# Splitting fp32 PE transposes into two 64-partition row tiles in a fused RG-LRU and soft-MoE kernel

## The chip, the cores and the metric

The kernel runs on one core of a Trainium2 chip (trn2). The metric is the device time of one execution in microseconds (us), on that core. A run gives one time; the median of several runs stands for a kernel. A profiled execution gives a trace beside it, whose span (first to last instruction) is a little shorter than the time.

## The reference

Everything is fp32. B, S, D = 4, 5056, 256, so there are 20224 tokens of 256 features; E = 8 experts with 4 slots each (32 slots) and a hidden width of 1024.

```
sig_r = sigmoid(r_gate);  sig_i = sigmoid(i_gate)
a_t   = exp(8 * sig_r * log(clip(sigmoid(a_param))))        # per token and feature
xg    = sqrt(max(1 - a_t*a_t, 1e-6)) * sig_i * x
h[t]  = a_t[t] * h[t-1] + xg[t];  y = h                     # scan over S, per batch row
logits = y @ phi                                            # 20224 x 32
slot_in = softmax(logits over tokens).T @ y                 # 32 x 256
slot_out[e] = relu(slot_in[e] @ w1[e]) @ w2[e]              # 4 slots of each expert
out = softmax(logits over slots) @ slot_out                 # 20224 x 256
```

## The kernel before

Tokens are taken in quads of 512 (40 of them, the last is half) and units of two quads (21 units, the first and the last of one quad). Loads bring a quad with tokens on partitions: partition p holds 4 consecutive tokens, 4 KB. The scan needs features on partitions and time along the free axis, so three kinds of PE transposes through an identity stand between the layouts:

- **TR** (`mk_sr`, line 857): the gate r of a quad, 8 transposes of 128x128 into a two-bank PSUM tile `pair`; ACT then computes tanh from it into the SBUF tile `A` (**SR**, line 868).
- **TU** (`mk_scan`, line 1013): u, the gated x of a unit, one feature half h at a time, 8 transposes (16 in the units marked E, where i and x are added up in PSUM) into a `pair`; DVE multiplies it by the norm in place (**ST**, line 1030) and scans (**SC**, line 1047), which writes y over `A`.
- **TY** (`mk_y`, line 1073): y back to tokens on partitions, 8 transposes a quad into a `pair`, copied by ACT (line 1087) or DVE (line 1089) to the SBUF tile `yn` (**YC**). The quads 37 to 39 go through `mk_yh` (line 1103) and quad 29 through one bank at a time.

Each transpose is one weight load (the data are the stationary operand) and one matmul (the identity streams): 128 columns in both. In the trace `pair<-ident,st` and `pair<-ident,b` at these three lines are the transposes; a `pair` is one of three, `one` is a single bank.

Other work on PE: **LG** (logits, line 1153), **TE/TF** (transposed logits, line 1197 and 1223), **AC** (slot sums, line 1251), **CT** (line 1627), **SP** and **DN** (slot inputs and denominators, lines 1474 and 1488), **L1/L2** (experts, lines 1529 and 1577), **HP/OT** (output, lines 1693 and 1721), and **WU**, fillers of two transposes of the identity (line 1402) which the planner puts where its plan has PE idle. ACT also does the gates' tanh or sigmoid **SI** (lines 907 and 909), **EX** (exp, line 975), **RT** (square root, line 994) and the exponentials of the softmax. POOL multiplies (lines 937 and 957). SP queues every load and store.

The order of tasks on each engine is a table of names, `ORDER`, walked by `run_fixed`, which keeps a clock with modelled durations only to give out buffers, to interleave the emission and to place fillers. So a task waits for the one before it on its engine, for its inputs, and for its buffer.

Of the kernel before, what the change touches and what calls it, by code (L numbers as in the profile page):

```python
# [16 lines left out]
P = 128  # L17
J = 4
# [138 lines left out]
COLD = 5.5  # L157
PEL = 0.21
# [424 lines left out]
def kernel(  # L583
# [188 lines left out]
    def load(nm, q):  # L772
# [5 lines left out]
        def emit():  # L778
            rows = src[nm][q * QT : q * QT + n * P, :].rearrange("(p n) d -> p (n d)", n=n)
# [63 lines left out]

    def mk_sr(q):
# [18 lines left out]
        tr = add("PE", f"TR{q}", 0.05 + 0.2182 * n, deps=[ld[("r", q)], t_const], prio=q - TRP, emit=e_tr,  # L863
                 alloc=[rp], uses=[st[("r", q)]], shape="T")
# [135 lines left out]
    def mk_scan(p):  # L1000
        c = plen(p)
        tok0 = quads(p)[0] * QT
        for h in range(H):
            up = Buf("pair", f"up{p}.{h}")

            def e_tu(h=h, up=up):
                for i, q in enumerate(quads(p)):
                    n = qlen(q) // P
                    o = inv(t(up)[:, i, : n * P], n)
                    nms = ("i", "x") if gate_of(q) == "E" else ("x",)  # L1010
                    for nm in nms:
                        for m in range(n):
                            nc.tensor.matmul(  # L1013
                                o[:, m, :],
                                raw(nm, q)[:, m * D + h * P : m * D + (h + 1) * P],
                                ident, is_transpose=True, start=(nm == nms[0] and m == 0), stop=(nm == nms[-1]),
                                skip_group_check=True,
                            )

            nt = 2 if gate_of(quads(p)[0]) == "E" else 1  # L1020
            tu = add("PE", f"TU{p}.{h}", 0.04 + 0.1091 * c / P * nt, deps=[U[q] for q in quads(p)], prio=pos_u(p) - TUP + h * 0.1,
                     emit=e_tu, alloc=[up], uses=[st[(nm, q)] for q in quads(p) for nm in (("x", "i") if nt == 2 else ("x",))],
                     shape="T")

            def flat(up=up):
                return t(up).rearrange("p a b -> p (a b)")
# [29 lines left out]
    def mk_y(q):  # L1056
# [6 lines left out]
        for b0 in range(0, qlen(q) // P, step):  # L1063
            yp = Buf("pair" if q in YP4 else ONE, f"yp{q}.{b0}")
# [726 lines left out]
```

## Time and profile before

| what | value |
|---|---|
| time, median of 3 runs | 288.57 us (287.92 to 288.71) |
| profiled execution, span | 286.4 us |
| busy PE / DVE / ACT / POOL | 257.5 / 229.0 / 238.8 / 192.7 us |
| DMA moved | 100.05 MB, mean 349 GB/s |
| mean granted PE clock | 0.988 |

The profiled execution was not timed apart from its span, so the median is the time that it is set beside: 2.2 us lie outside the span (288.57 - 286.4). The run has four stretches: gates, scan and everything behind them until about 207 us, the close of the softmax over tokens until 214, the experts (L1, L2) until 232, and the output until 286. Busy time on PE is the time covered by its matmuls, whose ends are modelled; spacing from one start to the next tells more. An engine's idle time is put down to what released it last.

### The profile page before, as it was taken

Reading aid. Unit: us, or ns where it says so; the run is one execution under the profiler, and the core shown is the slowest. Engines: PE = TensorE matmul, PEld = TensorE weight load, DVE = VectorE, ACT = ScalarE, POOL = GpSimd, SP = SyncE. Lnnn points to the kernel's source line nnn. Section 1 sums busy time; section 2 is a strip of 40 time slices with the busy share of each in tenths; the row PEclk is TensorE's granted clock in tenths of the full one; section 3 lists DMA queues with packets and bytes.
Section 4 is the critical chain, followed back from the end, with each engine's and each line's share of the span. In section 5 each row is a group of like instructions: output and inputs, shape, how many; then the busy total and the mean of one; then the engine's idle time right before and its main releaser. Section 6 shows DMA issues by size and latency. Waiting matters only on the chain.

```text
span 286.4 us, 6221 instructions
## 1 busy us (share of the span) xinstructions
PE 257.5 (90%) x2455; PEld 196.3 (69%) x2455; DVE 229.0 (80%) x269; ACT 238.8 (83%) x253; POOL 192.7 (67%) x148
## 2 busy tenths in 40 slices
PE   8889899989999879869998999999999999999850
PEld 7888767877767657556977766676765578777640
DVE  0148749999999899999999999999965558886730
ACT  7799999999999999999999999999542069955440
POOL 5198997999999999989999999993010511310100
PEclk9999999999999999999999999999999999999995
DMA  6999999999999929976999998799996039999996
GB/s 227 387 412 404 402 410 366 403 414 408 407 406 410 403 96 378 412 272 241 338 410 355 380 323 332 252 364 392 399 408 256 3 128 414 420 412 418 414 406 289
DMA packets 27409, 100.05 MB, mean 349 GB/s; under 512 B 3058, under 2 KB 3060, under 8 KB 24948
## 3 DMA queue, kind: packets, MB, share of 16 engines
q1 hardware_dynamic: 27376, 99.66, 89.0%
q8 instruction: 19, 0.31, 0.4%
q14 instruction: 10, 0.08, 0.1%
q10 hardware_dynamic: 4, 0.00, 0.0%
HBM read 78.94 MB, written 20.71 MB: 348 GB/s over the span
## 4 chain that ended last, share of the span: by engine, by line
PE 38%; ACT 19%; DMA 14%; DVE 13%; issue 9%; POOL 3%; SPq 2%; ACTq 0%; POOLq 0%; DVEq 0%
DMA st<-in_r_gate_dram 10%; PE bank L1721 6%; PE pair L1013 5%; ACT b L868 5%; ACT b L994 5%; PE pair L1073 4%; DVE b L1047 4%; DVE pair L1030 4%; ACT b L909 4%; DMA b<-in_x_dram 4%; PE one L1251 3%; PE bank L1529 3%; PE one L1577 2%; PE one L1153 2%; PE pair L857 2%
## 5 line engine op out<-in xcount | busy, mean ns | idle before, releaser
L1047 DVE TENSOR_TENSOR_SCAN b<-b,pair 128x1024 f32<-128x1024 f32 (+8 forms) x48 | 93.1, 1951 | 0.7
L937 POOL TENSOR_TENSOR b<-b 128x1024 f32<-128x1024 f32 x38 | 89.8, 2398 | 3.9 <-ACT b L909 2.8
L957 POOL TENSOR_TENSOR b<-b 128x1024 f32<-128x1024 f32 (+2 forms) x39 | 71.2, 1864 | 10.6 <-ACT b L975 10.6
L1013 PE MATMUL pair<-ident,b 128*128 128x128 f32 x412 | 52.5, 275 | 5.7 <-DVE b L1047 2.8
L1030 DVE SCALAR_TENSOR_TENSOR pair<-b,pair 128x1024 f32<-128x1024 f32 (+2 forms) x42 | 48.1, 1154 | 6.9 <-issue 2.9
L1013 PEld LDWEIGHTS pair<-ident,b 128*128 128x128 f32 x412 | 45.1, 140 | 11.8 <-DVE yn L1089 3.3
L857 PE MATMUL pair<-ident,st 128*128 128x128 f32 x308 | 40.7, 277 | 4.8 <-DMA st<-in_r_gate_dram 2.4
L975 ACT ACTIVATE b<-b,ca 128x2048 f32<-128x2048 f32 (+3 forms) x24 | 42.8, 1803 | 0.0
L1655 POOL TENSOR_TENSOR b<-b,rs_all 128x512 f32<-128x512 f32 (+3 forms) x12 | 10.6, 895 | 47.5 <-DVE rs_all L1650 17.7
L1073 PE MATMUL pair<-ident,b 128*128 128x128 f32 x288 | 38.8, 278 | 4.1 <-ACT b L868 1.9
L857 PEld LDWEIGHTS pair<-ident,st 128*128 128x128 f32 x308 | 33.7, 141 | 11.4 <-ACT b L868 5.1
L1073 PEld LDWEIGHTS pair<-ident,b 128*128 128x128 f32 x288 | 31.3, 140 | 13.3 <-DVE b L1047 3.2
L868 ACT ACTIVATE b<-pair 128x1024 f32<-128x1024 f32 (+1 forms) x39 | 38.3, 1010 | 1.7 <-PE pair L857 1.5
L1089 DVE COPY yn<-pair 128x1024 f32<-128x1024 f32 x23 | 27.7, 1206 | 3.0 <-PE pair L1073 3.0
L1735 ACT COPY b<-bank 128x512 f32<-128x512 f32 x35 | 19.5, 611 | 12.7 <-PE bank L1721 9.3
L1721 PE MATMUL bank<-eS,yn 32*128 32x256 f32 x238 | 27.2, 406 | 2.0 <-ACT b L1735 0.9
L994 ACT ACTIVATE b<-b 128x2048 f32<-128x2048 f32 (+1 forms) x14 | 25.2, 1820 | 0.0
L1721 PEld LDWEIGHTS bank<-eS,yn 32*128 32x128 f32 x238 | 19.3, 197 | 5.6 <-ACT b L1735 1.6
L909 ACT ACTIVATE b<-b 128x2048 f32<-128x2048 f32 x12 | 22.9, 1917 | 0.0
L1251 PE MATMUL one<-yn,eS 128*32 128x257 f32 x296 | 22.3, 385 | 0.0
L1153 PE MATMUL one<-b,phi_sb 128*32 128x512 f32 (+1 forms) x164 | 20.9, 579 | 0.0
L1737 DVE COPY b<-bank 128x512 f32<-128x512 f32 x22 | 14.4, 679 | 8.1 <-PE bank L1721 4.5
(152 smaller groups left out, 375.0 us busy)
## 6 DMA issues: line engine op xcount, KB each, us to landing
b<-in_x_dram SPq DMA_DIRECT2D x39, 512.0 KB, 9.1
st<-in_r_gate_dram SPq DMA_DIRECT2D x38, 512.0 KB, 8.1
b<-in_i_gate_dram SPq DMA_DIRECT2D x38, 512.0 KB, 7.7
out_dram<-b SPq DMA_DIRECT2D x19, 1024.0 KB, 6.9
b<-in_moe_w_dram SPq DMA_DIRECT2D x28, 512.0 KB, 7.5
st<-in_moe_w_dram SPq DMA_DIRECT2D x4, 512.0 KB, 6.0
st<-in_r_gate_dram SPq DMA_DIRECT2D x3, 256.0 KB, 2.8
st<-in_i_gate_dram SPq DMA_DIRECT2D x1, 512.0 KB, 6.3
```

The costliest lines, as they stand in the source:

```text
L857: nc.tensor.transpose(out=o[:, m, :], in_=raw("r", q)[:, m * D + h * P : m * D + (h + 1) * P], identity=ident,)
L868: nc.scalar.activation(dst, t(rp)[:, :, :c], AF.Sigmoid if SIGR else AF.Tanh, scale=1.0 if SIGR else 0.5)
L909: nc.scalar.activation(v, v, AF.Tanh, scale=0.5)
L937: eng.tensor_tensor(out=o, in0=a, in1=b, op=ALU.mult)
L957: eng.tensor_tensor(out=o, in0=v, in1=v, op=ALU.mult)
L975: nc.scalar.activation(v, v, AF.Exp, scale=ca[:, h : h + 1], bias=ca[:, h : h + 1])
L994: nc.scalar.activation(v, v, AF.Sqrt, bias=quarter if f != 1.0 else f, scale=-f)
L1013: nc.tensor.matmul(o[:, m, :], raw(nm, q)[:, m * D + h * P : m * D + (h + 1) * P], ident, is_transpose=True, start=(nm == nms[0] and m == ...
L1030: nc.vector.scalar_tensor_tensor(v, t(Nb[p])[:, h, :c], 0.5e-3 if gate_of(quads(p)[0]) == "E" else 1e-3, v, op0=ALU.max, op1=ALU.mult)
L1047: nc.vector.tensor_tensor_scan(dst, dst, flat()[:, s0:s1], init, op0=ALU.mult, op1=ALU.add)
L1073: nc.tensor.transpose(out=flat()[:, b * D + h * P : b * D + (h + 1) * P], in_=tokens(q, b0 + b, 1)(h), identity=ident,)
L1721: nc.tensor.matmul(t(ops[x])[:, c * D : (c + 1) * D], t(hT)[r, off : off + (P - 1) * ns + 1 : ns], t(soRb)[r, :D], start=True, stop=True,)
```

## The change

Each transpose of TR (but quad 0), TU and TY (but the quads in single banks) becomes two: the upper 64 partitions of the data against a 64x64 identity, and the lower 64, one after the other, each writing 64 columns. The two halves go to different banks of the `pair`. To make that possible, layouts move: in a unit of two quads, x and i are loaded with 8 tokens to a partition (a quad's load takes 4 of them, so 4 KB out of every 8 KB); ACT's SR and the copies YC read and write with one more dimension; and `yn` holds the features in the order (f, h, k) in place of (h, f, k), so SP is split into matmuls that write 64 partitions each and waits for both halves of the last update of `accS` (AE11a and AE11b) in place of the first alone. Engine orders in `ORDER` are the same; the planner's modelled durations differ, so fillers and buffers move.

```
+TT = 0.0655
+HP = 64
...
-            rows = src[nm][q * QT : q * QT + n * P, :].rearrange("(p n) d -> p (n d)", n=n)
+            if nm != "r" and len(quads(p)) == 2:
+                u0 = quads(p)[0] * QT
+                rows = src[nm][u0 : u0 + plen(p), :].rearrange("(p n) d -> p (n d)", n=2 * J)[:, i * J * D : (i + 1) * J * D]
+            else:
+                rows = src[nm][q * QT : q * QT + n * P, :].rearrange("(p n) d -> p (n d)", n=n)
...
+    def rowtiles(in_):
+        for f in range(2):
+            k = slice(f * HP, (f + 1) * HP)
+            yield f, in_[k], ident[k, k]
...
             for h in range(H):
-                o = inv(t(rp)[:, h, :c], n)
+                o = [inv(t(rp)[:, f, h * c // 2 : (h + 1) * c // 2], n) for f in range(2)]
                 for m in range(n):
-                    nc.tensor.transpose(
-                        out=o[:, m, :],
-                        in_=raw("r", q)[:, m * D + h * P : m * D + (h + 1) * P],
-                        identity=ident,
-                    )
+                    for f, v, idn in rowtiles(raw("r", q)[:, m * D + h * P : m * D + (h + 1) * P]):
+                        nc.tensor.transpose(out=o[f][:, m, :], in_=v, identity=idn)
...
         def e_sr():
-            dst = t(A[p])[:, :, i * QT : i * QT + c]
-            nc.scalar.activation(dst, t(rp)[:, :, :c], AF.Sigmoid if SIGR else AF.Tanh, scale=1.0 if SIGR else 0.5)
+            dst = t(A[p])[:, :, i * QT : i * QT + c].rearrange("q h (f x) -> q h f x", f=2)
+            v = t(rp)[:, :, :c].rearrange("q f (h x) -> q h f x", h=H)
+            nc.scalar.activation(dst, v, AF.Sigmoid if SIGR else AF.Tanh, scale=1.0 if SIGR else 0.5)
...
+                n = c // P
+                o = [inv(t(up)[:, 0, QT - c // 2 :], n), inv(t(up)[:, 1, : c // 2], n)]
...
+                            for f, v, idn in rowtiles(raw(nm, q)[:, m * D + h * P : m * D + (h + 1) * P]):
+                                nc.tensor.matmul(
+                                    o[f][:, i * J + m, :], v, idn, is_transpose=True,
...
+                        for f, v, idn in rowtiles(tokens(q, b0 + b, 1)(h)):
+                            nc.tensor.transpose(out=t(yp)[:, f, (b * H + h) * HP : (b * H + h + 1) * HP], in_=v, identity=idn)
...
+                if wide:
+                    dst = dst.rearrange("p j (f d) -> p f j d", f=2)
+                    v = t(yp)[:, :, : nb * P].rearrange("p f (j d) -> p f j d", d=P)
...
         def e_sp(h):
-            nc.tensor.matmul(
-                t(sp)[:, h * NS : (h + 1) * NS], accS[:, h * P : (h + 1) * P], small["W"][:, 0, :],
-                start=True, stop=True,
-            )
-
-        a = add("PE", "SP0", 0.26, deps=[w, AE["a"]], prio=-60, alloc=[sp], emit=lambda: e_sp(0), shape="M")
+            for f in range(2):
+                nc.tensor.matmul(
+                    t(sp)[f * HP : (f + 1) * HP, h * NS : (h + 1) * NS],
+                    accS[:, f * P + h * HP : f * P + (h + 1) * HP], small["W"][:, 0, :], start=True, stop=True,
+                )
+
+        a = add("PE", "SP0", 0.26, deps=[w, AE["a"], AE["b"]], prio=-60, alloc=[sp], emit=lambda: e_sp(0), shape="M")
```

PE near the start, from TR0 (`one<-ident,st`, two halves) over TR1 to TR2; `pair<-ident` and `one<-ident` without a second name are fillers. Before:

```order
L882 MATMUL one_78<-ident,st_61 128x128 x4
L1402 MATMUL pair_83<-ident 128x128 x2
L1402 MATMUL pair_84<-ident 128x128 x2
L857 MATMUL pair_82<-ident,st_62 128x128 x8
L1402 MATMUL one_77<-ident 128x128 x2
L1402 MATMUL pair_83<-ident 128x128 x2
L1402 MATMUL one_78<-ident 128x128 x2
L857 MATMUL pair_84<-ident,st_63 128x128 x8
```

and with the change:

```order
L892 MATMUL one_78<-ident,st_61 128x128 x4
L1418 MATMUL pair_83<-ident 128x128 x2
L1418 MATMUL pair_84<-ident 128x128 x2
L870 MATMUL pair_82<-ident,st_62 128x64 x16
L1418 MATMUL one_77<-ident 128x128 x2
L1418 MATMUL pair_83<-ident 128x128 x2
L1418 MATMUL one_78<-ident 128x128 x2
L1418 MATMUL pair_84<-ident 128x128 x2
L870 MATMUL pair_83<-ident,st_63 128x64 x16
```

Eight transposes have become sixteen of half the height, and one more filler stands ahead of TR2.

PE at the close of the softmax over tokens, from the last AC over CT3, SP0, DN, SP1 and CT4 to L1 (`yn,eS` is AC, `ident,b` CT, `W,accS` SP, `accS,W` DN, `b,yn` L1). Before:

```order
L1251 MATMUL bank_2142<-yn_70,eS_76 32x257 x2
L1627 MATMUL bank_2146<-ident,b 128x4x32 x4
L1474 MATMUL one_77<-W,accS 128x32
L1488 MATMUL one_77<-accS,W 128x1
L1474 MATMUL one_77<-W,accS 128x32
L1627 MATMUL bank_2141<-ident,b 128x4x32 x4
L1529 MATMUL bank_2145<-b,yn_71 32x256 x32
```

and with the change:

```order
L1267 MATMUL bank_3184<-yn_70,eS_76 32x257 x2
L1644 MATMUL bank_3188<-ident,b 128x4x32 x4
L1491 MATMUL one_78<-W,accS 64x32 x2
L1505 MATMUL one_78<-accS,W 128x1
L1491 MATMUL one_78<-W,accS 64x32 x2
L1644 MATMUL bank_3183<-ident,b 128x4x32 x4
L1546 MATMUL bank_3187<-b,yn_71 32x256 x32
```

SP0 and SP1 have become two matmuls of 64 output partitions each, on either side of DN, which keeps 128. Up to there the whole list of PE changes its tile shape 120 times in place of 58 and holds 67 fillers in place of 54.

## Rows read from the trace of the kernel before

**Rows 1.** Busy us of PE, PEld, DVE, ACT, POOL by stretch; clock, DMA share, GB/s

```profile
10.00:201.00 191.00, 176.80 (x1572) 136.83 (x1572) 172.85 (x142) 190.25 (x154) 175.50 (x97) 1.00 0.94 362
201.00:214.40 13.40, 13.38 (x148) 9.43 (x140) 10.48 (x26) 7.27 (x13) 1.69 (x3) 1.00 1.03 404
...
232.00:286.40 54.40, 41.77 (x423) 32.68 (x419) 35.51 (x74) 31.41 (x67) 6.11 (x7) 0.94 0.93 382
```

**Rows 2.** What ACT waited for, 9 to 206 us: total us, times, longest

```profile
ACT yn L1087 <- PE pair L1073: 1.5, 1, 1.5
ACT b L868 <- PE pair L857: 1.5, 1, 1.5
```

**Rows 3.** What DVE waited for, 43 to 208 us

```profile
DVE pair L1030 <- ACT b L994: 1.3, 3, 0.8
DVE pair L1030 <- PE pair L1013: 1.1, 4, 0.4
```

**Rows 4.** Groups of PE transposes: shapes, count, busy us, mean ns, idle before

```profile
L1013 PE MATMUL pair<-ident,b 128*128 128x128 f32 x412 | 52.5, 275 | 5.7 <-DVE b L1047 2.8 <-DVE yn L1089 1.7 <-ACT b L868 0.9
L857 PE MATMUL pair<-ident,st 128*128 128x128 f32 x308 | 40.7, 277 | 4.8 <-DMA st<-in_r_gate_dram 2.4 <-ACT b L868 1.5 <-DVE b L1047 0.4
L1073 PE MATMUL pair<-ident,b 128*128 128x128 f32 x288 | 38.8, 278 | 4.1 <-ACT b L868 1.9 <-DVE b L1047 1.7 <-ACT yn L1087 0.3
```

**Rows 5.** One TY within the chain that ended last: start, us on the chain

```profile
182.42 0.87 PE pair L1073 x8
```

**Rows 6.** Timeline of PE: four transposes of 32 partitions, and what follows

```profile
39.20 0.43 PE L1197 MATMUL one<-ident,b 32*128 32x32 f32 x4
39.56 1.42 PE L1013 MATMUL pair<-ident,b 128*128 128x128 f32 x11
```

**Rows 7.** The same transposes on line 1197: ns min/median/max, and their loads' timeline

```profile
L1197 PE MATMUL one<-ident,b x32: 221/273/330, 39.2 to 175.0; 128*128 128x128 f32 x28, 32*128 32x32 f32 x4
39.20 0.32 PEld L1197 LDWEIGHTS one<-ident,b 32*128 32x128 f32 x4 [0.17 <-issue]
```

**Rows 8.** Weight loads of OT: four loads into four row tiles; their group

```profile
243.09 0.21 PEld L1721 LDWEIGHTS bank<-eS,yn 32*128 32x128 f32 x4 [0.27 <-DVE b L1737]
L1721 PEld LDWEIGHTS bank<-eS,yn 32*128 32x128 f32 x238 | 19.3, 197 | 5.6 <-ACT b L1735 1.6 <-DVE b L1641 1.1 <-ACT yn L1704 1.0
```

**Rows 9.** Timeline near the start: PE's TR2 and ACT's SR2

```profile
8.88 1.09 PE L857 MATMUL pair<-ident,st 128*128 128x128 f32 x8 [0.91 <-DMA st<-in_r_gate_dram]
10.01 1.03 ACT L868 ACTIVATE b<-pair 128x1024 f32<-128x1024 f32 x1 [1.46 <-PE pair L857]
```

**Rows 10.** Timeline at the end of the scans: DVE's ST19, SC20; PE's LG11

```profile
196.96 2.36 DVE L1030 SCALAR_TENSOR_TENSOR pair<-b,pair 128x1024 f32<-128x1024 f32 x2 [0.34 <-PE pair L1013]
206.34 0.75 DVE L1047 TENSOR_TENSOR_SCAN b<-b,pair 128x256 f32<-128x256 f32 x1
207.19 0.52 PE L1153 MATMUL bank<-b,phi_sb 128*32 128x128 f32 x6
```

**Rows 11.** Timeline of the close: DVE's AE11, PE's SP0, DN, SP1, CT4, L1

```profile
212.68 0.61 DVE L1285 SCALAR_TENSOR_TENSOR accS<-accS,dm,bank 128x128 f32<-128x128 f32 x2 [0.50 <-PE bank L1251]
213.15 0.34 PE L1474 MATMUL one<-W,accS 128*128 128x32 f32 x2
213.35 0.38 PE L1488 MATMUL one<-accS,W 128*128 128x1 f32 x2
213.59 0.39 PE L1474 MATMUL one<-W,accS 128*128 128x32 f32 x2
213.81 0.70 PE L1627 MATMUL bank<-ident,b 128*128 128x128 f32 x4
214.45 0.42 PE L1529 MATMUL bank<-b,yn 128*32 128x256 f32 x4
```

**Rows 12.** ACT reading PSUM: SR from 9 us on, and SR0 in pieces of two

```profile
L868 ACT ACTIVATE b<-pair x38: 602/1021/1062, 10.0 to 175.1; 128x1024 f32<-128x1024 f32 x37, 128x512 f32<-128x512 f32 x1
L892 ACT ACTIVATE b<-one 128x512 f32<-128x512 f32 x2 | 1.3, 634 | 0.1
```

More of the change, by code (lines that the diff above doesn't have):

```diff
@@ L1006, in e_tu @@
             def e_tu(h=h, up=up):
+                n = c // P
+                o = [inv(t(up)[:, 0, QT - c // 2 :], n), inv(t(up)[:, 1, : c // 2], n)]
                 for i, q in enumerate(quads(p)):
[L1008 to L1009 removed]
                     nms = ("i", "x") if gate_of(q) == "E" else ("x",)
                     for nm in nms:
[L1012 to L1018 removed]
+                        for m in range(qlen(q) // P):
+                            for f, v, idn in rowtiles(raw(nm, q)[:, m * D + h * P : m * D + (h + 1) * P]):
+                                nc.tensor.matmul(
+                                    o[f][:, i * J + m, :], v, idn, is_transpose=True,
+                                    start=(nm == nms[0] and m == 0 and i == 0), stop=(nm == nms[-1]),
+                                    skip_group_check=True,
+                                )
             nt = 2 if gate_of(quads(p)[0]) == "E" else 1
[L1021 removed]
+            tu = add("PE", f"TU{p}.{h}", 0.04 + TT * c / P * nt, deps=[U[q] for q in quads(p)], prio=pos_u(p) - TUP + h * 0.1,
                      emit=e_tu, alloc=[up], uses=[st[(nm, q)] for q in quads(p) for nm in (("x", "i") if nt == 2 else ("x",))],
[L1023 removed]
+                     shape="H")
             def flat(up=up):
[L1026 removed]
+                return t(up).rearrange("p a b -> p (a b)")[:, QT - c // 2 : QT + c // 2]
             def e_st(h=h, flat=flat):
@@ L1063, in mk_y @@
         for b0 in range(0, qlen(q) // P, step):
-            yp = Buf("pair" if q in YP4 else ONE, f"yp{q}.{b0}")
+            wide = q in YP4
+            yp = Buf("pair" if wide else ONE, f"yp{q}.{b0}")
             nb = min(step, qlen(q) // P - b0)
@@ L1068, in flat, with e_ty, e_yc @@
                 return t(yp).rearrange("p a b -> p (a b)") if yp.tags == ("pair",) else t(yp)
-            def e_ty(b0=b0, flat=flat, nb=nb):
+            def e_ty(b0=b0, flat=flat, nb=nb, yp=yp, wide=wide):
                 for b in range(nb):
                     for h in range(H):
-                        nc.tensor.transpose(
-                            out=flat()[:, b * D + h * P : b * D + (h + 1) * P],
-                            in_=tokens(q, b0 + b, 1)(h),
-                            identity=ident,
-                        )
-            ty = add("PE", f"TY{q}.{b0}", 0.04 + 0.2182 * nb, deps=[SC[(p, h)] for h in range(H)],
+                        if not wide:
+                            o = flat()[:, b * D : (b + 1) * D].rearrange("p (f h k) -> p h f k", f=2, h=H)[:, h]
+                            nc.tensor.transpose(out=o, in_=tokens(q, b0 + b, 1)(h), identity=ident)
+                            continue
+                        for f, v, idn in rowtiles(tokens(q, b0 + b, 1)(h)):
+                            nc.tensor.transpose(out=t(yp)[:, f, (b * H + h) * HP : (b * H + h + 1) * HP], in_=v, identity=idn)
+            ty = add("PE", f"TY{q}.{b0}", 0.04 + 2 * (TT if wide else 0.1091) * nb, deps=[SC[(p, h)] for h in range(H)],
                      prio=q - 1 + (YLAG if q < NQ - YEND else 0) + b0 * 0.1, emit=e_ty, alloc=[yp] + ([yn[q]] if b0 == 0 else []),
-                     uses=[A[p]] + ([yn[q]] if b0 else []), shape="T")
-            def e_yc(b0=b0, flat=flat, nb=nb):
+                     uses=[A[p]] + ([yn[q]] if b0 else []), shape="H" if wide else "T")
+            def e_yc(b0=b0, flat=flat, nb=nb, yp=yp, wide=wide):
                 dst = t(yn[q]).rearrange("p (j d) -> p j d", d=D + 1)[:, b0 : b0 + nb, :D]
                 v = flat()[:, : nb * D].rearrange("p (j d) -> p j d", d=D)
+                if wide:
+                    dst = dst.rearrange("p j (f d) -> p f j d", f=2)
+                    v = t(yp)[:, :, : nb * P].rearrange("p f (j d) -> p f j d", d=P)
                 if planner.cur.eng_used == "ACT":
```

12 lines of the change are left out of this document (6 added, 6 removed).

## The prediction

> **What bounds the kernel now.** I read the busy time by stretch first, then what ACT and DVE waited for, then PE where its work ends last. In the stretch from 10 to 201 us ACT is busy 190.25 of 191.00 us; DVE has 172.85, PE 176.80, POOL 175.50, and the DMA engines 94% [rows 1]. The reader is to see that four resources are nearly full, and that one of them, ACT, has no gap. Its waits say the same: from 9 to 206 us ACT waited for PE twice, 1.5 us each, and for nobody else [rows 2]. The first is at 10.01 us, for TR2, which itself waited for its load until 8.88 [rows 9]; the second falls behind 201 us. DVE, once it is full, waited four times for TU, 1.1 us in all, and three times for ACT's square roots, 1.3 us in all [rows 3]. PE's idle time lies in many pieces behind ACT, DVE and loads [rows 4]: a faster PE mostly waits longer for them. Only from 201 to 214.4 us is PE the full one (13.38 of 13.40) while ACT has 7.27 and DVE 10.48 [rows 1]; the order there is fixed, and the last scan ends at 207.09 [rows 10], so what counts is when DVE gets there and the chain behind it. After 232 us the DMA engines are at 93% with 382 GB/s, and that stretch only moves with its start [rows 1].
>
> **The change part by part.**
>
> *What a pair of halves costs on PE.* A transpose of 128 columns costs 0.109 us in a run of eight (0.87 / 8) [rows 5]; 412 + 308 + 288 = 1008 of those in the trace are in the three groups that change [rows 4]. No transpose of 64 partitions in a row tile by the side of another is in the trace. The nearest are four transposes of 32 partitions with 32 columns to stream and 128 columns to load: they take 0.43 us, the shortest matmul 0.221, so their starts are 0.07 apart ((0.43 - 0.221) / 3) [rows 6, 7]. They share one row tile, so a load of 128 columns with a short matmul costs no more than 0.07. The streaming of 64 columns should cost half of 0.109, 0.055. Whether two row tiles load side by side is shown by OT: four loads into four row tiles take 0.21 us together where one takes 0.197 on average [rows 8], so they start within about 0.02 us. I take 0.065 for a pair, between 0.055 and 0.07, since it is nearest to these rows; the low end is 0.055, the high end 0.14, two loads one after the other. The saving is 0.044 us a transpose (from -0.031 to 0.054), 44 us over 1008.
>
> [...]
>
> *What it adds on PE.* A change of tile shape costs about 0.08: the last of the four small ones starts at 39.41 (39.20 + 0.43 - 0.221) and the next transpose at 39.56, 0.15 later in place of 0.07 [rows 6, 7]. The list has 120 changes in place of 58: 62 x 0.08 = 5 us. Thirteen more fillers at two transposes: 13 x 0.22 = 2.9 us. PE's net is 44 - 5 - 3 = 36 us less. Nearly all lies beside ACT's unbroken work and counts nothing; if that cover went (ACT lighter by 14 us, PE's idle time from 10 to 201), it would begin to count.
>
> *The start of ACT.* TR2 is eight transposes behind a load that lands at 8.88; ACT's SR2 waits for them, and from there on ACT has no gap. 8 x 0.044 = 0.35 us earlier (from -0.25 to 0.43). The extra filler ahead of TR2 (0.22 us) fits into the 0.91 us that PE waits for the load [rows 9]. This shift goes through to 201 us, unless a load or POOL holds ACT up in between: then that is late next.
>
> *DVE's waits for TU.* Of the 1.1 us [rows 3] I count only the last wait, 0.34 us before 196.96 [rows 10], since ACT's square roots hold DVE three times after earlier ones, and those move with ACT alone. TU19 with half the time is done before ACT's root, so 0.34 us (from 0 to 1.1).
>
> *From 201 to 212.7 us.* LG11 needs the last scan, which ends at 207.09 [rows 10]; the other tasks there speed up in step with ACT (TY35, TY36) or are unchanged, so no further term. I take 0.
>
> *SP.* Four matmuls in place of two, in another tile shape than DN between them, and SP0 now waits for both AE11 updates. These end at 213.29 (212.68 + 0.61), DN begins at 213.35, SP0 at 213.15 [rows 11]. So SP0 begins 0.2 later, and DN stands a whole SP0 (0.2) and a change (0.08) behind it, then another change: SP1 would begin near 213.35 + 0.2 + 0.08 + 0.24 + 0.08 = 213.95 in place of 213.59. Behind SP on PE are CT4 and L1 (214.45), and DVE's copy of the slot inputs waits for it too [rows 11]; nothing covers this. I take 0.35 us, from 0 (the waits overlap) to 0.6.
>
> *Loads, copies and SR.* The strided loads move the same 4 KB a partition in the same number of DMAs; from 201 to 214.4, when loads of w2 in steps are among those in flight, the engines still move 404 GB/s [rows 1]. I take nothing; if they were slower, POOL's products would be late, and ACT behind them. SR reads four pieces of 256 in place of two of 512, YC writes eight runs of 128 in place of four of 256: nothing by the plain rows, but SR0, which writes pieces of two elements, takes 634 ns where 512 elements take 602 otherwise [rows 12]. That gives the upper end, 0.032 us an instruction, and it would stand on ACT, which has no slack.
>
> *Sum.* -0.35 - 0.34 + 0.35 = -0.34 us against the profiled execution, span 286.4; 2.2 us lie outside it, which nothing here touches. Against the median, 288.57 - 0.34 = **288.2 us**. By its own bounds this case runs from 287.6 to 288.9.
>
> **The rivals.**
>
> *Faster: PE's waits all count.* The four waits of DVE for TU and the start of ACT go, and the split of SP hides behind AE11: 288.57 - 0.35 - 1.1 = 287.1 (286.4 to 287.7). For it: the waits are there [rows 3], and PE is full where the kernel turns to the close [rows 1]. Against: between them DVE waits for ACT.
>
> *Slower: ACT's new access patterns.* 38 SR [rows 12] and 13 YC on ACT at up to 0.032 us more are 51 x 0.032 = 1.6 us on the engine without a gap: 288.2 + 1.6 = 289.8. It turns the sign from 0.34 / 51 = 0.007 us an instruction, and is measurably slower from 0.024. For it: every ns on ACT counts. Against: pieces of two elements cost 0.032, pieces of 256 should cost far less.
>
> *The halves don't run side by side.* At 0.109 a pair PE has 8 us more from fillers and changes, most of it in 14 us of idle time [rows 1]; with some in the full stretch at the end about 290. At 0.14 it is 31 + 8 = 39 us more work, 14 of them hidden: 313. The change would then not do what it says. Against: OT's loads [rows 8].
>
> *The clock falls.* A PE that waits more could lose its granted clock; it is 1.00 from 10 to 214 us and 0.94 at the end, where PE is busy 41.77 of 54.40 [rows 1]. [...] Against: the last stretch has long waits and keeps most of its clock. [...]
>
> **How the numbers follow.** The forecast has 0.47, the faster rival 0.28, ACT's patterns 0.13, the halves 0.08, the clock 0.04. About 0.3% (0.87 us, so below 287.70 or above 289.44) is what a measurement of this kernel can tell from no change. Faster: 0.27 of the first rival and 0.06 of the forecast, 0.33. Slower: 0.08 + 0.04 + 0.09 of ACT's patterns and 0.01 of the forecast, 0.22. The rest, 0.45, is the same. The range reaches from the low end of the faster rival, with a little for waits that I don't see, to ACT's patterns with 0.6 for a dearer SP, 286.2 to 290.4; left out are the clock and most of the halves, and about 0.05 at the ends.
>
> **What would show it.** Right: a run of sixteen halves takes about 0.5 us in place of 0.87; PE's busy time falls and its idle time behind ACT and DVE grows; ACT is still without a gap from about 9.7 to 200.6; SR takes 1021 ns and DVE's YC what it took; SP0 to L1 is longer by about 0.35. Wrong: sixteen halves take 0.87 or more; a clock below 1.00 before 201 us; SR or YC longer by 20 ns; ACT waiting for a load or for POOL; or a close that shrinks by more than 0.5 us.

## The result, and the profile after

The changed kernel took 292.12 us (median of 4 runs, 291.49 to 293.06), the kernel before beside it 288.38 us (287.92 to 288.71). The ratio is 1.0129, 95% interval 1.0102 to 1.0155: slower by 3.7 us. The prediction said 288.2, in a range from 286.2 to 290.4; the measured time lies above it.

Busy time by stretch in the profile after (PE, PEld, DVE, ACT, POOL, then clock, DMA share, GB/s), as in [rows 1]:

```profile
10.00:201.00 191.00, 149.19 (x2523) 105.25 (x2523) 168.43 (x140) 187.37 (x150) 175.38 (x97) 0.94 0.94 356
201.00:214.40 13.40, 13.04 (x190) 8.07 (x193) 11.94 (x22) 8.13 (x17) 1.69 (x3) 1.00 1.04 401
232.00:289.80 57.80, 45.80 (x456) 34.75 (x448) 35.87 (x76) 32.79 (x72) 7.40 (x9) 0.91 0.87 359
```

In the long stretch PE is 27.6 us lighter than before, but ACT, which was busy 190.25 of 191.00 us, is now busy 187.37, so it has 3.6 us of gaps. Two more numbers moved that should have stood still: the clock of that stretch is 0.94 in place of 1.00, and at the same DMA share (0.94) the engines moved 356 GB/s in place of 362.

The transposes themselves, by group (shapes, count, busy us, mean ns, idle time before), against [rows 4]:

```profile
L1024 PE MATMUL pair<-ident,b 64*128 64x64 f32 x824 | 36.8, 235 | 14.3 <-DVE b L1057 4.8 <-ACT b L878 3.7 <-POOL b L947 2.9
L870 PE MATMUL pair<-ident,st 64*128 64x64 f32 x616 | 28.6, 238 | 14.4 <-DMA st<-in_r_gate_dram 6.5 <-ACT b L878 2.5 <-DVE b L1057 2.2
L1089 PE MATMUL pair<-ident,b 64*128 64x64 f32 x576 | 26.2, 233 | 10.1 <-DVE b L1057 4.6 <-ACT b L878 2.9 <-ACT yn L1102 1.7
```

They fell from 132.0 to 91.6 us in all, and the idle time before them rose from 14.6 to 38.8 us. The work went, and PE waited in its place.

What ACT waited for from 9 to 210 us (us in all, times, longest):

```profile
ACT b L878 <- PE pair L870: 2.9, 4, 1.2
ACT yn L1102 <- PE pair L1089: 1.1, 1, 1.1
ACT b L878 <- POOL b L947: 0.8, 1, 0.8
ACT b L919 <- DMA b<-in_i_gate_dram: 0.5, 1, 0.5
```

Before, only two waits for PE stood there [rows 2]. Of these, 2.9 us for PE fall into four waits (TR, for SR), and two waits are new in kind: for POOL and for a load. These places in ACT's timeline (start, us, line, operation, and in brackets the idle time and its releaser), after first and then the same operations before (the first of them is in [rows 9]):

```profile
9.73 1.03 ACT L878 ACTIVATE b<-pair 128x1024 f32<-128x1024 f32 x1 [1.25 <-PE pair L870]
...
33.45 1.91 ACT L919 ACTIVATE b<-b 128x2048 f32<-128x2048 f32 x1 [0.52 <-DMA b<-in_i_gate_dram]
...
107.48 1.03 ACT L878 ACTIVATE b<-pair 128x1024 f32<-128x1024 f32 x1 [0.83 <-POOL b L947]
...
133.16 1.02 ACT L878 ACTIVATE b<-pair 128x1024 f32<-128x1024 f32 x1 [0.33 <-PE pair L870]
...
137.08 1.03 ACT L878 ACTIVATE b<-pair 128x1024 f32<-128x1024 f32 x1 [1.10 <-PE pair L870]
```

```profile
32.85 1.92 ACT L909 ACTIVATE b<-b 128x2048 f32<-128x2048 f32 x1
...
105.83 1.01 ACT L868 ACTIVATE b<-pair 128x1024 f32<-128x1024 f32 x1
...
130.92 1.01 ACT L868 ACTIVATE b<-pair 128x1024 f32<-128x1024 f32 x1
...
133.62 1.03 ACT L868 ACTIVATE b<-pair 128x1024 f32<-128x1024 f32 x1
```

The order of ACT's operations is the same in both, so the difference of two starts is the lag of the whole kernel at that place: -0.28 us at the start (10.01 before [rows 9]), +0.60 at 33 us, behind a load of i (of the lead 0.04 was left at 25.22 us, where another load of i landed at 25.20 in place of 24.74), +1.65 at 107 us, behind POOL, +2.24 and +3.46 at 133 and 137 us, behind PE. POOL's lateness is a load again. Its timeline near 98 us, after and before:

```profile
98.10 4.69 POOL L947 TENSOR_TENSOR b<-b 128x1024 f32<-128x1024 f32 x2 [2.16 <-DMA st<-in_r_gate_dram]
```

```profile
95.45 4.71 POOL L937 TENSOR_TENSOR b<-b 128x1024 f32<-128x1024 f32 x2 [0.63 <-DMA b<-in_x_dram]
```

The product waits 2.16 us where it waited 0.63, and starts 2.65 us later. The profile puts the wait down to a load of r; the x tile that the product reads landed at 97.97 us, where it had landed at 95.32 before.

The other two places, at 133 and 137 us, are PE's. Windows of after, columns as above:

```profile
57.50:64.30 6.80, 3.82 (x96) 3.27 (x96) 6.11 (x6) 6.76 (x6) 6.72 (x5) 1.00 1.02 413
64.30:71.13 6.83, 6.13 (x79) 4.87 (x80) 6.52 (x5) 6.83 (x5) 6.83 (x5) 0.50 1.03 411
...
91.50:98.40 6.90, 3.99 (x84) 3.21 (x84) 6.90 (x8) 6.88 (x6) 4.74 (x4) 1.00 1.02 407
98.40:105.30 6.90, 5.48 (x68) 3.46 (x68) 5.21 (x5) 6.86 (x6) 6.90 (x4) 0.51 0.57 228
...
119.00:125.70 6.70, 4.25 (x80) 2.82 (x76) 6.09 (x7) 6.67 (x5) 6.70 (x5) 1.00 1.03 417
125.70:136.00 10.30, 8.33 (x84) 5.06 (x84) 8.89 (x8) 9.93 (x8) 9.15 (x6) 0.50 0.57 205
```

Three times, for 24 us together, the granted clock was 0.50, the lower of the two levels in this trace (1.00 and 0.50), each time behind a stretch in which PE had been busy 3.8 to 4.3 us of some 6.8. In the same three stretches of before PE was busy 5.66, 5.48 and 5.25 us, and the clock stayed at 1.00. That share doesn't decide it alone: the kernel before was as lightly busy from 120.2 to 127 us and kept its clock, and e10, below, lost it behind a stretch with more work.

```profile
120.20:127.00 6.80, 4.30 (x43) 3.05 (x36) 6.80 (x7) 6.78 (x7) 6.76 (x5) 1.00 0.81 313
```

At 137 us the low clock is what ACT waits for: the logits ahead of that TR, after and then before, take 3.35 us where they took 1.92.

```profile
133.04 3.35 PE L1169 MATMUL one<-b,phi_sb 128*32 128x512 f32 x16
```

```profile
130.28 1.92 PE L1153 MATMUL one<-b,phi_sb 128*32 128x512 f32 x16
```

So the trace of after offers two causes: loads of i and x that land later, and a low clock. It doesn't say which of them the time hangs on, since the later tasks of a late kernel wait for less. **Theory A**: the halves leave PE too little work, its clock falls, and TR and TU come late. **Theory B**: the loads at a pitch are slower. **Theory C**: 1046 more PE instructions need more instruction fetches (27 packets of 16 KB on that queue in place of 19), which hold up the loads.

### The profile page after: what moved, and what is told of

The parts are those of the page before. It is cut to its first block, busy times and chain, and to the rows that moved or that the text cites. A ratio compares the mean times of both kernels' runs of the same rounds, so it can differ in the third digit from the quotient of the medians.

```text
span 289.8 us, 8311 instructions
## 1 busy us (share of the span) xinstructions
PE 233.8 (81%) x3501; PEld 165.9 (57%) x3501; DVE 227.5 (79%) x269; ACT 239.6 (83%) x253; POOL 192.6 (66%) x148
## 4 chain that ended last, share of the span: by engine, by line
PE 25%; DMA 21%; ACT 20%; POOL 17%; issue 7%; DVE 6%; SPq 1%; ACTq 0%; POOLq 0%; DVEq 0%
DMA b<-in_x_dram 11%; DMA st<-in_r_gate_dram 10%; POOL b L947 8%; POOL b L967 7%; PE bank L1738 7%; ACT b L985 5%; ACT b L1004 3%; ACT b L878 3%; ACT yn L1102 3%; PE bank L1546 2%; PE one L1594 2%; DVE b L1057 2%; PE pair L1024 2%; PE pair L870 2%; PE one L1169 1%
## 5 line engine op out<-in xcount | busy, mean ns | idle before, releaser
L1024 PE MATMUL pair<-ident,b 64*128 64x64 f32 x824 | 36.8, 235 | 14.3 <-DVE b L1057 4.8
L1024 PEld LDWEIGHTS pair<-ident,b 64*128 64x128 f32 x824 | 30.9, 145 | 23.0 <-issue 7.1
L870 PE MATMUL pair<-ident,st 64*128 64x64 f32 x616 | 28.6, 238 | 14.4 <-DMA st<-in_r_gate_dram 6.5
L870 PEld LDWEIGHTS pair<-ident,st 64*128 64x128 f32 x616 | 23.9, 148 | 22.5 <-DVE b L1057 4.9
L1089 PE MATMUL pair<-ident,b 64*128 64x64 f32 x576 | 26.2, 233 | 10.1 <-DVE b L1057 4.6
L1089 PEld LDWEIGHTS pair<-ident,b 64*128 64x128 f32 x576 | 21.5, 143 | 19.8 <-DVE b L1057 5.7
L1104 DVE COPY yn<-pair 128x1024 f32<-128x1024 f32 x23 | 27.8, 1207 | 3.7 <-PE pair L1089 3.7
L1267 PE MATMUL one<-yn,eS 128*32 128x257 f32 x296 | 24.2, 408 | 0.6 <-ACT yn L1102 0.3
L1169 PE MATMUL one<-b,phi_sb 128*32 128x512 f32 (+1 forms) x164 | 22.5, 618 | 0.0
```

The lines of the kernel that those rows point to most:

```text
L870: nc.tensor.transpose(out=o[f][:, m, :], in_=v, identity=idn)
L1024: nc.tensor.matmul(o[f][:, i * J + m, :], v, idn, is_transpose=True, start=(nm == nms[0] and m == 0 and i == 0), stop=(nm == nms[-1]), ski ...
L1089: nc.tensor.transpose(out=t(yp)[:, f, (b * H + h) * HP : (b * H + h + 1) * HP], in_=v, identity=idn)
L1104: nc.vector.tensor_copy(out=dst, in_=v)
```

## Experiments

A ratio is against the kernel before in the same set of runs; 0.001 is 0.29 us.

| run | what it is | us | ratio, 95% |
|---|---|---|---|
| e1 | TR in halves alone | 288.55 | 1.0004, 0.9979 to 1.0029 |
| e2 | TU in halves, loads at a pitch | 291.55 | 1.0104, 1.0074 to 1.0134 |
| e3 | TY in halves, SP split | 288.59 | 1.0035, 1.0006 to 1.0064 |
| e4 | before, x and i loads at a pitch | 290.49 | 1.0081, 1.0055 to 1.0106 |
| e18 | before, x loads at a pitch | 289.24 | 1.0031, 1.0008 to 1.0054 |
| e9 | after, loads as before | 289.23 | 1.0036, 1.0012 to 1.0060 |
| e10 | e9, more PE work | 289.89 | 1.0051, 1.0031 to 1.0070 |
| e17 | TR and TU in halves, loads as before | 288.99 | 1.0014, 0.9992 to 1.0036 |
| e13 | after, loads of 1 MB | 291.62 | 1.0104, 1.0066 to 1.0142 |
| e14 | e13 without TY and SP | 292.73 | 1.0109, 1.0053 to 1.0164 |
| e15 | before, loads of 1 MB | 290.39 | 1.0070, 1.0045 to 1.0095 |
| e16 | halves at the two ends, loads of 1 MB there | 289.26 | 1.0022, 1.0000 to 1.0045 |

### One part of the change at a time (e1 to e4)

e1 takes from the diff only TR and SR:

```
 before.py + e_tr, e_sr of the change; TR's planned time 0.05 + 2 * TT * n
```

> Halves in the gate transposes (TR) alone; loads, TU, TY and SP as before. Theory A (TensorE's clock falls because the halves leave it too little work): one third of the saved work is not enough, granted clock 1.00 in all stretches before 201 us, and the time is the kernel before less the earlier start of ScalarE (0.28 us in the trace of after at 23 us): 287.9 to 288.4. Theory B (the strided x and i loads land late): no such loads here, the same 287.9 to 288.4. Theory C (more PE instructions, so more instruction fetches on the DMA engines that hold up the loads): 308 instructions more of the 1046 that the change adds, about a third of the 1.2 to 2.6 us by which loads came late: 288.5 to 289.2.

Measured 288.55 us, no difference. The number lies at the low end of C's range and 0.15 us above that of A and B; the interval (287.8 to 289.2) covers both, so this run doesn't decide. The clock fell once, for 3.4 us near 129 us, where A had it at 1.00, and the mean of the long stretch is 0.99. Nothing is lost that can be measured, and nothing won either: the earlier start of ACT doesn't reach the end.

e2 takes TU and the loads it needs, e3 takes TY and SP:

```
 before.py + the loads of x and i and e_tu of the change
 before.py + e_ty, e_yc, mk_yh and e_sp of the change
```

> Halves in the u transposes (TU) alone, with the strided x and i loads that they need; TR, TY and SP as before. Theory A: clock 1.00 before 201 us in all or nearly all stretches, time of the kernel before less what VectorE gains at the end (0.45 us): 287.9 to 288.4. Theory B: the loads are those of after, so x lands 1.2 us late by 70 us and 2.6 us late by 94 us as in after, and the time is 289.5 to 291. Theory C: 412 instructions more, some 40 per cent of the lateness: 288.5 to 289.3.

> Halves in the y transposes (TY) alone, with the SP product in two column halves; loads, TR and TU as before. Theory A: clock 1.00 before 201 us, the SP split costs 0.36 us as in the trace of after: 288.5 to 288.9. Theory B: the same 288.5 to 288.9. Theory C: 288 instructions more, 288.8 to 289.5.

e2 took 291.55 us, above all three ranges and nearest to B's. e3 took 288.59 us, where A and B had it; by its ratio it is 1.0 us slower (0.2 to 1.8), of which SP's split is a part, and that would fit C as well. In both the clock fell before 201 us (three times and once, 3.4 us each). So C is left to e4 and e9.

e4 changes no transpose at all. Its diff is the change's own lines on the load:

```
+            if nm != "r" and len(quads(p)) == 2:
+                u0 = quads(p)[0] * QT
+                rows = src[nm][u0 : u0 + plen(p), :].rearrange("(p n) d -> p (n d)", n=2 * J)[:, i * J * D : (i + 1) * J * D]
+            else:
                 rows = ...
```

> The kernel before with the strided x and i loads alone (the tokens then stand in another order within a pair of tiles, so u is taken at other tokens than the gates; the work is the same). Theory A: same as the kernel before, 288.1 to 288.8, clock 1.00 before 201 us, loads landing as before. Theory B: loads late by 1.2 us at 70 us and 2.6 us at 94 us, time 289.5 to 291. Theory C: no instruction more, 288.1 to 288.8.

290.49 us: B, and neither A nor C, since PE's instructions and its clock are those of before. Windows of e4 (first two rows), then of before and of after:

```profile
10.00:201.00 191.00, 174.53 (x1534) 135.59 (x1532) 170.30 (x141) 188.27 (x150) 175.60 (x97) 1.00 0.95 358
...
110.00:140.00 30.00, 26.15 (x230) 19.21 (x229) 29.02 (x26) 29.90 (x25) 28.99 (x17) 1.00 0.88 304
```

```profile
110.00:140.00 30.00, 26.74 (x234) 19.88 (x235) 29.26 (x27) 29.95 (x24) 28.58 (x17) 1.00 0.85 331
```

```profile
110.00:140.00 30.00, 22.56 (x356) 14.54 (x358) 27.44 (x26) 28.50 (x23) 28.68 (x17) 0.83 0.85 297
```

With a clock of 1.00 ACT has lost 2 us, and the DMA engines are busier from 110 to 140 us (0.88 against 0.85) while they move less (304 against 331 GB/s). Moved per busy share that is 304 / 0.88 = 345 against 389 GB/s; after has 297 / 0.85 = 349. POOL's waits from 85 to 160 us, e4 and then before:

```profile
POOL b L941 <- DMA b<-in_x_dram: 2.7, 3, 1.2
```

```profile
POOL b L937 <- DMA b<-in_x_dram: 0.6, 1, 0.6
```

Single packets of that stretch differ too. The trace has a time for each 4 KB packet; over the packets that start between 95 and 140 us, in ns:

```
                          median   90th pct   99th pct
before                       159        168        449
e1  (loads as before)        159        167        371
e3  (loads as before)        159        167        419
e9  (loads as before)        159        168        695
e17 (loads as before)        159        167        433
after (x, i at a pitch)      159        226        493
e2  (x, i at a pitch)        159        192        651
e4  (x, i at a pitch)        159        246        569
e18 (x at a pitch)           159        218        647
```

Most packets take 159 ns everywhere. In this stretch the slowest tenth begins at 192 to 246 ns in the four kernels with loads at a pitch and at 167 or 168 ns in the five without. Landed means here that all packets of a load are in, so a few slow ones could make it late. That they do is not shown: e9 has the highest 99th percentile of all, and from 45 to 95 us, where the x load of 97.97 us fell behind, the 90th is 167 to 169 ns in all nine kernels and only the 99th differs (291 to 342 ns with a pitch, 190 to 272 without). What e4 shows is the price of such loads, not how they come to be late.

### Which loads (e18)

```
-            if nm != "r" and len(quads(p)) == 2:
+            if nm == "x" and len(quads(p)) == 2:
```

> e4 with the x loads alone at a pitch of 8 KB, those of i in one unbroken piece as before. If each load at a pitch is later by about the same: half of e4's 2.1 us, 289.0 to 289.8. If it is the x loads that count, since GpSimd waits for x last: 289.9 to 291. If those of i, for which ScalarE waits at 33 us: 288.1 to 288.9.

0.31% slower (0.08 to 0.54), 0.9 us: the first case. The x loads make somewhat under half of e4's loss; the rest falls to those of i by difference, since no run has them alone.

### The change with the loads of before (e9, e10, e17)

e9 is the changed kernel with the lines of e4's diff taken back out.

> The changed kernel with the loads of the kernel before (each 512 KB in one unbroken piece); the u transposes are left as they are, so the tokens of u come out in another order than the gates'; the work is the same. Theory A + B (2.1 us of the 3.7 come from the strided loads as e4 measured, some 1 us from the low clock, 0.4 from SP): clock low in two or three stretches before 201 us, 289.3 to 290.5. If the strided loads cost their 2.1 us only together with e4's full transposes: 291.5 to 292.5. If the low clock costs nothing: 288.0 to 288.9.

289.23 us, just under the range for A + B, and 0.36% over before (0.12 to 0.60): 1.0 us remain of 3.7, so the loads are worth 2.7 us by this way and 2.3 by e4's (each give or take about 1 us). Windows of e9:

```profile
10.00:201.00 191.00, 149.40 (x2539) 107.49 (x2537) 169.78 (x141) 187.55 (x150) 175.44 (x97) 0.94 0.93 356
...
110.00:140.00 30.00, 22.29 (x388) 15.75 (x390) 28.33 (x26) 29.70 (x24) 26.91 (x16) 0.87 0.79 295
```

The clock is as low as in the changed kernel, 0.94, and ACT of this profiled execution (290.68 us, above the median) has as many gaps. Moved per share, 295 / 0.79 = 373 GB/s, it is nearer to before's 389 than to e4's 345; the low 295 itself comes from loads that are issued later here. In its trace ACT waits up to 1.3 us at once for TR, at 50 us, right behind a low stretch, as it does 1.10 us in the changed kernel. So the low clock costs waits. That these are nearly the whole loss of the change, as theory A has it, is out: with the same clock the kernel is 2.7 us faster. Nor does the clock fall only behind the lightest stretches: before its fall at 42.9 us PE had been busy 5.11 of 6.80 us.

e10 gives PE more to do, ahead of the y transposes:

```
             def e_ty(...):
+                for _ in range(8 if wide and q < 25 else 0):
+                    nc.tensor.transpose(out=t(yp)[:, 0, :P], in_=ident, identity=ident)
```

> e9 with 8 whole transposes of the identity ahead of each y transpose task of the tiles 0 to 24 (0.87 us of extra TensorE work each, before the wait for VectorE's scan, into the banks that the task fills next anyway). Theory A (the low clock costs about 1 us): clock 1.00 before 201 us and 0.6 to 1.5 us under e9: 288.0 to 289.3. If the low clock costs nothing: as e9, or up to 1 us above it, since the extra work delays some transposes.

Windows of e10:

```profile
122.10:128.90 6.80, 5.18 (x93) 4.19 (x86) 6.34 (x6) 6.78 (x6) 5.63 (x4) 1.00 0.70 265
125.70:136.00 10.30, 8.48 (x153) 6.04 (x150) 9.89 (x11) 10.05 (x10) 9.12 (x7) 0.83 0.48 161
```

The mean clock from 10 to 201 us rose to 0.98, two short falls remain in place of five (at 19.7 and 128.9 us, the second right behind the first row above), and the time is 289.89 us: not better, the case in which the low clock costs nothing. The extra transposes delay those behind them by what the clock gives back, or the clock is worth little; this run doesn't tell these apart.

e17 is e9 with TY and SP as before.

> e9 with the y transposes and SP as in the kernel before: halves in the gate and the u transposes alone, with the old loads (the tokens of u in another order than the gates'). Theory: the 0.8 us of e9 over the kernel before are 0.36 us of SP and the low clock, less what ScalarE gains at the start and VectorE at the end; here SP's part is gone and TensorE has about 20 us more work, so fewer stretches at the low clock: 287.9 to 288.7. If the low clock or the halves cost more than that: 288.8 to 289.6, as e9 or above.

0.14% over before (-0.08 to 0.36): no difference that can be measured, with a clock of 0.96 from 10 to 201 us; the median lies in the upper of the two ranges, and the interval reaches into both. Halves in TR and TU win or lose nothing measurable. What is left in e9 beyond that, some 0.6 us (-0.3 to 1.6 by the two intervals), fits SP's split, which takes 0.36 us in the trace of after (below), but isn't shown to be it.

### Other ways to load (e5 to e8, e11 to e16)

Halves of a bank need the tokens of 64 partitions to be neighbours. I tried to get this with unbroken pieces. In e5 and e7 each load is two pieces of 256 KB, in e6 16 pieces of 32 KB:

```
-  .rearrange("(p n) d -> p (n d)", n=2 * J)[:, i * J * D : (i + 1) * J * D]
+  .rearrange("(g i b n) d -> i g b (n d)", g=P // BLK, i=2, n=J)[i]      # BLK = 64 (e5, e7, e8) or 8 (e6)
```

> The kernel before with the x and i loads of a pair of tiles in another order again: each load of 512 KB is two unbroken pieces of 256 KB (64 partitions each) where the changed kernel has 128 pieces of 4 KB at a pitch of 8 KB. As in e4 the tokens of u then stand at other places than the gates', the work is the same. Theory B1 (it is the many small pieces that are slow): loads and time as before, 288.0 to 289.0. Theory B2 (any departure from one unbroken piece, or the two loads of a pair sharing one region): 289.5 to 291 as in e4 (290.49).

> As e5 with pieces of 32 KB (8 partitions) at a pitch of 64 KB. Theory B1, if the pitch of 8 KB between neighbouring packets is what is slow: as before, 288.0 to 289.0. If the cost grows with the number of pieces: between, 288.4 to 289.5. Theory B2: 289.5 to 291.

> The changed kernel whole, all transposes in halves and SP in two column halves, but with the loads of e5 and the u transposes written for that order of tokens (the two halves of a bank's rows then come out in the order of the tokens). Theory A + B (2.1 us of the 3.7 from the strided loads, the rest from the low clock and SP): clock low in two or three stretches as in the changed kernel, 289.3 to 290.5. If the low clock itself costs nothing: 288.2 to 288.9. If B1 is wrong: 291.5 to 292.5.

> e7 with 8 whole transposes of the identity ahead of each y transpose task of the tiles 0 to 24 (0.87 us of extra TensorE work each, before the wait for VectorE's scan, into the bank that the task fills next anyway). Theory A (low clock costs about 1 us): clock 1.00 before 201 us, 0.7 to 1.5 us under e7: 288.0 to 289.3. If the low clock costs nothing: as e7 or up to 1 us above it, since the extra work delays some transposes.

They took 964.02, 369.72, 963.07 and 962.65 us, far above every range, and tell nothing of the pitch, since each form of load has a much larger cost of its own. From the DMA view of e5 (packets and rate; queue, packets, MB, share of 16 engines):

```profile
DMA packets 26345, 100.05 MB, mean 104 GB/s; under 512 B 1994, under 2 KB 1996, under 8 KB 23884
...
q1 hardware_dynamic: 26312, 99.65, 28.7%
```

The same bytes take 28.7% of the 16 engines' span of 962 us, at 104 GB/s in place of 349: taken over the whole span, the engines have no packet for most of it. The trace doesn't name the engines, and why such loads are slow isn't shown.

e11 writes the same two pieces as two DMAs of 64 partitions, and e12 does so only for the last two pairs of tiles, with halves only where after had won time (TR1, TR2, the last three units' TU):

```
+                for f in range(2):
+                    t0 = (quads(p)[0] + f) * QT + i * QT // 2
+                    rows = src[nm][t0 : t0 + QT // 2, :].rearrange("(p n) d -> p (n d)", n=n)
+                    held(dst[f * HP : (f + 1) * HP, : n * D], rows)
```

> The changed kernel whole and with the reference's order of tokens, each x or i load of a pair of tiles issued as two loads of 256 KB, each one unbroken piece into 64 partitions, in place of 128 pieces of 4 KB at a pitch of 8 KB; the u transposes are written for that order. If 64 partitions are filled at the same rate per load as 128: as e9, 289.3 to 290.5. If they are filled more slowly, or SyncE's twice as many issues come late: 291 to 300.

> Halves only where the trace of the changed kernel gains from them: the gate transposes of tiles 1 and 2 (ScalarE's start, 0.3 us) and the u transposes of the last three units (VectorE's end, 0.45 us); x and i of units 18 and 19 in two loads of 256 KB each; all else, SP too, as before. Clock 1.00 before 201 us. 287.4 to 288.2 if both gains last to the end; 288.2 to 288.9 if they are taken back by the loads (start) and by VectorE's other work (end).

377.65 and 297.32 us, ratios 1.307 and 1.031: misses too. In e11 a 4 KB packet takes 279 ns (median) in place of 159, 279 / 159 = 1.75 times as long, and from 45 to 95 us the DMA engines move 234 GB/s at a share of 1.01, before 404 at 1.02; what makes these packets slow isn't shown. The eight such tiles of e12 made ACT wait 5.2 us for one TR and 2.5 us for one load of i.

In e13 to e15 each pair of tiles is one load of 1 MB, 8 KB unbroken into each partition, which leaves the tokens as the change has them:

```
+                if i == (nm == "i"):
+                    u0 = quads(p)[0] * QT
+                    held(t(b).rearrange("p a b -> p (a b)"), src[nm][u0 : u0 + plen(p), :].rearrange("(p n) d -> p (n d)", p=P))
```

> The changed kernel whole, with the reference's order of tokens, but each pair of x or i tiles in one load of 1 MB (8 KB unbroken into each partition, the same places in the tile as now) in place of two loads of 128 pieces of 4 KB at a pitch of 8 KB. Theory B (the pieces at a pitch are what comes late): as e9, 288.6 to 289.8. If loads as large as that come late by themselves (the first tile of a pair waits for the whole 1 MB, 1.3 us more): 290 to 291. If the loads are not the main cause: 291.5 to 292.5.

> e13 without the halves in the y transposes and without the split of SP (both as in the kernel before). Theory A + B: 0.36 us of SP less and more TensorE work, so fewer stretches at the low clock: 0.4 to 1.0 us under e13, 288.0 to 289.2. If neither counts: as e13.

> The kernel before with the loads of e13 and nothing else (the tokens of u then stand at other places than the gates'). Theory B: as the kernel before, 288.0 to 289.0, against 290.49 of the two loads at a pitch in e4. If loads of 1 MB cost by themselves: 289.3 to 290.5.

e15 is 0.70% slower (0.45 to 0.95), as slow as e4 within the intervals, so loads of 1 MB cost by themselves, some 2.0 us. e13 (1.04%) came out where it was to come out if the loads were not the main cause; with loads that cost 2.0 us themselves it can't tell. e14 (1.09%) isn't under e13, as was expected of it. Moved per busy share from 110 to 140 us these loads are as good as before's:

```profile
45.00:95.00 50.00, 48.07 (x408) 37.27 (x408) 49.49 (x44) 49.86 (x35) 47.46 (x27) 1.00 0.97 390
110.00:140.00 30.00, 26.15 (x229) 19.34 (x230) 29.34 (x26) 29.95 (x25) 28.11 (x17) 1.00 0.88 347
```

347 / 0.88 = 394 GB/s in e15, against 389 before and 345 in e4. What the 1 MB loads lose must be something else; that the first tile of a pair now waits for the second would be one, but no run here shows it. So it stays open whether unbroken loads of the usual size, in this order of tokens, would save the change.

e16 is e12 with such 1 MB loads in its place:

> Halves only where the trace of the changed kernel gains from them, as in e12, but with the x and i of units 18 and 19 in one load of 1 MB each: the gate transposes of tiles 1 and 2 (ScalarE's start, 0.3 us) and the u transposes of the last three units (VectorE's end, 0.45 us); all else as before. Clock 1.00 before 201 us. Theory: both gains last, 287.4 to 288.1; if they are taken back by the loads at the start and by VectorE's other work at the end: 288.1 to 288.8.

289.26 us, above both ranges; 0.22% slower (0.00 to 0.45), not faster. No version here beats the kernel before.

## Why the prediction was wrong

**What a pair costs: right.** 0.065 us was taken. One run of 16 halves in PE's timeline of after:

```profile
171.90 0.71 PE L1089 MATMUL pair<-ident,b 64*128 64x64 f32 x16
```

Its first two pairs start 0.11 us apart in the trace, behind another tile shape; with the last matmul's 0.22 us taken off, (0.71 - 0.22 - 0.11) / 6 = 0.063 us are left for each of the other steps. The two halves of a pair start some 4 ns apart, so they do run side by side. The sign "about 0.5 us" for such a run in place of 0.87 was read on the chain; in the timeline eight whole transposes take 1.09 [rows 9], and 1.09 - 0.71 is 0.047 a transpose, 0.044 said. PE's net saving from 10 to 201 us is 27.6, with 36 said; part of that time ran at the low clock.

**The start of ACT: right at its place, gone later.** SR2 began 0.28 us earlier (0.35 said). "This shift goes through to 201 us, unless a load or POOL holds ACT up in between" is how it went: ACT waits for loads of i, at 25.22 us and at 33.45.

**SR and YC: right.** SR takes 1020 ns (1021 before [rows 12]), YC on ACT 1016 (1014) and on DVE 1207 (1206). The rival of ACT's access patterns falls.

**DVE's last wait: right.** ST19, which waited 0.34 us for PE before [rows 10], waits for nobody:

```profile
199.97 2.36 DVE L1040 SCALAR_TENSOR_TENSOR pair<-b,pair 128x1024 f32<-128x1024 f32 x2
```

The lag falls from 3.46 to 3.0 us until the last scan, which ends at 210.09 (207.09 before [rows 10]); 0.34 was said.

**SP: right.** The close after, against [rows 11]:

```profile
215.68 0.61 DVE L1301 SCALAR_TENSOR_TENSOR accS<-accS,dm,bank 128x128 f32<-128x128 f32 x2 [0.50 <-PE bank L1267]
216.24 0.40 PE L1491 MATMUL one<-W,accS 128*64 128x32 f32 x4
216.58 0.38 PE L1505 MATMUL one<-accS,W 128*128 128x1 f32 x2
216.89 0.31 PE L1491 MATMUL one<-W,accS 128*64 128x32 f32 x4
217.13 0.75 PE L1644 MATMUL bank<-ident,b 128*128 128x128 f32 x4
217.81 2.57 PE L1546 MATMUL bank<-b,yn 128*32 128x256 f32 x42
```

From the end of AE11 to L1 it is 217.81 - 216.29 = 1.52 us, before 214.45 - 213.29 = 1.16: 0.36 us more, 0.35 said.

**The loads: the step that failed.** "The strided loads move the same 4 KB a partition in the same number of DMAs [...] I take nothing." The runs price this at 2.3 us (e4) to 2.7 us (after against e9), some two thirds of the loss. The reason given was a rate of 404 GB/s from 201 to 214.4 us, while loads of w2 in steps are among those in flight. But a rate over many loads says nothing of the last packet of each, and in that stretch nobody waits for a load. What follows in that sentence, "if they were slower, POOL's products would be late, and ACT behind them", is what happened. It had the way from a late load to ACT, but no price and no chance for it: four engines at 90% and more stood in [rows 1], and the DMA engines at 94%, so a term that touches them needed a range on the side of a loss. Two of the prediction's own signs of being wrong came true with it: ACT waited for a load and for POOL, and the clock was below 1.00 before 201 us. How a load at a pitch comes to be late stays open.

**The clock: given 0.04, and it fell.** The range left its time out, and no run shows what a fall for the whole stretch would cost. What came were three falls to 0.50, of 7 to 10 us, each back at 1.00 behind it. A clock of 0.50 for that time (the logits above take 3.35 us in place of 1.92), on an engine with a fifth of idle time (149.19 of 191.00 us busy), costs only the waits that it causes: 0.33 and 1.10 us in ACT's timeline above. e9 and e17, with such falls, come out 1.0 and 0.4 us over before, with SP's split in the first. So it is of the order of 1 us; a single number can't be taken from these runs, since the gains at both ends, and whatever the moved fillers and buffers do (no run has them alone), lie in the same sums.

In the lag along ACT and the close the sum of after is: -0.3 (start) + 0.9 (i load) + 1.05 (x load, through POOL) + 1.8 (PE, at the low clock) - 0.45 (DVE) + 0.36 (SP) = 3.4 us, the difference of the two spans, 289.8 and 286.4. The experiments divide it otherwise, more to the loads (2.3 to 2.7) and less to the clock. A lag is put down to the wait that came last at that place, and the engines behind a late load have other waits taken from them; what each cause is worth only the runs without it show. Theory C falls as the main cause, with e4, which loses its 2.3 us without one instruction more, and with e9, which has the 1046 instructions and the 27 packets of the changed kernel and loses 1.0: one of these packets begins at 91.0 us in either trace, and the x load that landed at 95.32 us before lands 2.65 us later in after and 0.16 earlier in e9. A part of that 1.0 it may have.

## What to carry to other kernels

A change that speeds up an engine off the critical path can only pay at places where that engine is waited for, while each thing it needs elsewhere (another order of the data, hence other loads) is paid on resources that are full: price those first, and give them a range even if bytes and descriptor sizes are unchanged. A load counts as landed with the last of its packets, so look at landings and late packets, not at mean rates. TensorE made faster without more to do can also lose clock, as in three stretches here (0.50 for 24 us together); read the clock by short stretches, not as a mean.

## What the runs showed of the hardware

- Packets of 4 KB at a pitch of 8 KB: median unchanged (159 ns), the 90th percentile from 168 to 192 to 246 ns between 95 and 140 us, hardly changed between 45 and 95 us (167 to 169 ns either way). Such loads of x and i cost a kernel with the DMA engines 94% busy 2.3 us of 288 (e4). Why was not found.
- TensorE's granted clock fell to 0.50 three times, for 7 to 10 us, in the middle of a kernel whose longest idle time on PE from 10 to 201 us is 2.5 us, behind stretches with 3.82 of 6.80, 3.99 of 6.90 and 4.25 of 6.70 us busy, and came back to 1.00 each time; it also fell behind 5.18 of 6.80 (e10) and held behind 4.30 of 6.80 (before), so this share alone doesn't tell; from 136 to 172 us it stayed at 1.00, with PE busy 27.6 us, 18.8 of them in the three groups that changed.
- Loads of 512 KB written as 2 x 64 rows (e5): 104 GB/s over the whole kernel in place of 349. Loads into 64 partitions (e11): 279 ns a packet in place of 159. Why isn't shown.
- Two fp32 transposes of 64 partitions each, of the upper and the lower half, to two banks: a pair every 0.063 us, the two some 4 ns apart, where a whole 128x128 one takes 0.109 us (0.87 / 8).
